# Three phases of d_ff chunks instead of two, with stores on ScalarE's queue, in a fused attention and softplus kernel

## Chip, cores, metric

One core of one Trainium2 chip. The metric is device time of one execution in microseconds, median of several runs. A single-core program gives no second core to compare with; each trace lists the granted TensorE clock.

Names: PE is TensorE, PEld its weight loads, ACT is ScalarE, DVE is VectorE, SP is SyncE (here only a queue of DMA issues). Of the tiles, `hp` takes a step's first product, `g` is its softplus, `gv` and `xv` are the three parts of g and of x, `op` takes the sums of the second product and `ot` is a copy of them; in attention `tp` is q turned (copied to `qT`), then come `kv` and `o`, and `xp` is x turned, with `xg` its scaled copy.

## The reference, cut to what matters

```python
kv  = einsum('bhsd,bhse->bhde', k, v)           # 8 batches, 8 heads, 576 rows, 64 wide
out = einsum('bhsd,bhde->bhse', q, kv)
x   = (out / rms(out) * g_norm) -> 4608 rows x 512
h   = x @ w_in                                  # 512 x 2048
g   = softplus(h)
return g @ w_out                                # 2048 x 512
```

The weights come as float64. The kernel rebuilds float32 values from their two words and carries every matmul operand as three parts, so that three matmuls stand for one in float32.

## The kernel before

36 tiles of 128 rows make 12 blocks of 384 rows. d_ff is 16 chunks of 128, in two phases of 8. One step is one chunk of one block: 12 matmuls into `hp`, softplus and split of its result on ACT and DVE, and, two steps later, 9 matmuls into three sums. All engines follow this program order.

```python
def mm1(ph, n, c):                    # 12 matmuls into hp
    ...
    nc.scalar.activation(g, hp, func=AF.Softplus, scale=1.0 + E)
    nc.scalar.activation(gv[:, 0], g, func=AF.Copy, scale=DOWN)
    nc.vector.tensor_tensor(out=gv[:, 1], in0=g, in1=f32[:, 0], op=ALU.subtract)
    nc.vector.scalar_tensor_tensor(out=gv[:, 2], ...)

def mm2(ph, n, c):                    # 9 matmuls into sums; at the last chunk of the phase:
    ...
    if ph == 0:
        ot = tmp.tile([P, d_model], F32, tag="ot", name="ot")     # 2 buffers, 3 tiles a block
        nc.scalar.activation(ot, sums[i], func=AF.Copy, scale=1.0 + E)
        nc.sync.dma_start(out=pdram[t], in_=ot)
    else: ...                         # sum + stored first sum, on DVE, to the output

def split_x(ph, t, x):                # three parts of a tile of x: ACT, DVE, DVE
    nc.scalar.activation(xv[:, 0], x, func=AF.Copy, scale=DOWN)
    nc.vector.tensor_tensor(out=xv[:, 1], in0=x, in1=f32[:, 0], op=ALU.subtract)
    nc.vector.scalar_tensor_tensor(out=xv[:, 2], ...)

def behind(step):
    mm2(*where(step - LAG))
    ...                               # i: chunk of 8; for the block that comes next
    if i in (0, 2, 4): load_x(n * TB + i // 2)
    if i in (2, 4, 6): split_x(ph, t, xts.pop(t))

def divide(j, w):                     # three parts of 128 x 512 weights
    nc.scalar.activation(dst[:, 0], w, func=AF.Copy, scale=DOWN)
    yield
    nc.vector.tensor_tensor(out=d, in0=w, in1=f32[:, 0], op=ALU.subtract)
    nc.scalar.activation(dst[:, 1], d, func=AF.Copy, scale=RADIX)
    yield
    nc.tensor.matmul(wd, lhsT=ident_r, rhs=dst[:, 0], start=True, stop=False)
    nc.tensor.matmul(wd, lhsT=minus_r, rhs=dst[:, 1], start=False, stop=True)
    nc.scalar.activation(dst[:, 2], wd, func=AF.Copy, scale=-E / (1.0 + E))

for step in range(CH, LAST):          # steps that still carry attention and conversion
    before(step)                      # mm1
    advance(heads, 1 + step % 2)      # pieces of attention: q transposed, kv, o, x transposed
    advance(weights, 1 + step % 2)    # stages of the weight conversion
    behind(step)                      # mm2, split, load
```

Attention's turned tiles of x are stored (`xg` to DRAM) and loaded again block by block (`xt`). PSUM leaves attention three places; one holds `kv`, so `xp` (x turned) and the next `tp` (q turned) want the same one.

Of the kernel before, what the change touches and what calls it, by code (L numbers as in the profile page):

```python
# [26 lines left out]
def kernel(  # L27
# [20 lines left out]

    nc = tc.nc
# [10 lines left out]
    CH = KF // 2  # L60
# [12 lines left out]
    ps_a = first_stack.enter_context(tc.tile_pool(name="ps_a", bufs=3, space=PSUM))  # L73
    att = first_stack.enter_context(tc.tile_pool(name="att", bufs=2))
    conv = first_stack.enter_context(tc.tile_pool(name="conv", bufs=1))

    ident_r = const.tile([P, P], F32R, name="ident_r")
    minus_r = const.tile([P, P], F32R, name="minus_r")
# [81 lines left out]
    def factors(j):  # L160
        c, of_out = divmod(j, 2)
        dst = wts.tile([P, 3, d_model], F32R, tag=f"w{of_out}_{c % CH}", name=f"w{of_out}_{c % CH}")
        (w_out_r if of_out else w_in_r)[c] = dst
        return dst, dst.bitcast(F32)

    def divide(j, w):
# [9 lines left out]
        wd = ps_h.tile([P, d_model], F32, tag="h", name="wd")  # L176
        nc.tensor.matmul(wd, lhsT=ident_r, rhs=dst[:, 0], start=True, stop=False)
        nc.tensor.matmul(wd, lhsT=minus_r, rhs=dst[:, 1], start=False, stop=True)  # L178
        nc.scalar.activation(dst[:, 2], wd, func=AF.Copy, scale=-E / (1.0 + E))
# [6 lines left out]
    def redivide(j):  # L186
# [4 lines left out]
        e = late.tile([P, d_model], F32, tag="e", bufs=2, name="e")  # L191
# [3 lines left out]
        yield  # L195
        nc.vector.scalar_tensor_tensor(out=e, in0=d, scalar=-RADIX, in1=f32[:, 0], op0=ALU.mult, op1=ALU.add)  # L196
        nc.scalar.activation(dst[:, 1], d, func=AF.Copy, scale=RADIX)  # L197
        yield
        nc.scalar.activation(dst[:, 2], e, func=AF.Copy, scale=-E / (1.0 + E))  # L199
# [77 lines left out]
    def turn_x(t):  # L277
# [4 lines left out]
        xg = att.tile([P, KD, P], F32, tag="xg", bufs=1, name="xg")  # L282
        nc.scalar.activation(xg, tp, func=AF.Identity, scale=g_col)  # L283
        xd[t] = dram.tile([P, KD * P], F32, name=f"x{t}")
        nc.sync.dma_start(out=xd[t], in_=xg.rearrange("p a t -> p (a t)"))
# [79 lines left out]
    def mm2(ph, n, c):  # L365
        gv, w = gvs.pop((ph, n, c)), w_out_r[c]
        first, last = c % CH == 0, c % CH == CH - 1
        for i in range(TB):
# [6 lines left out]
            if last:  # L375
                t = n * TB + i
                if ph == 0:
                    ot = tmp.tile([P, d_model], F32, tag="ot", name="ot")
                    nc.scalar.activation(ot, sums[i], func=AF.Copy, scale=1.0 + E)  # L379
                    pdram[t] = dram.tile([P, d_model], F32, name=f"part{t}")  # L380
                    nc.sync.dma_start(out=pdram[t], in_=ot)
                else:
                    ot = late.tile([P, d_model], F32, tag="ot", bufs=4, name="ot")
                    nc.vector.scalar_tensor_tensor(out=ot, in0=sums[i], scalar=scale, in1=parts_in.pop(t),  # L384
                                                   op0=ALU.mult, op1=ALU.add)
                    nc.sync.dma_start(out=out[t * P:(t + 1) * P], in_=ot)

    def load_part(t):
        parts_in[t] = late.tile([P, d_model], F32, tag="pt", bufs=3, name="pt")
        nc.sync.dma_start(out=parts_in[t], in_=pdram[t])  # L390


    HALF = n_blocks * CH
    STEPS = 2 * HALF

# [4 lines left out]
    def where(step):  # L400
        ph, r = divmod(step, HALF)
        n, c = divmod(r, CH)
        return ph, n, ph * CH + c

    def before(step):
        if step < STEPS:
            mm1(*where(step))

    def behind(step):
        if LAG <= step < STEPS + LAG:  # L410
            mm2(*where(step - LAG))

        m, i = divmod(step, CH)
        ph, n = divmod(m + 1, n_blocks)
        if ph < 2:
            if i in (0, 2, 4):
                load_x(n * TB + i // 2)
            if i in (2, 4, 6):
                t = n * TB + i // 2 - 1
                split_x(ph, t, xts.pop(t))  # L420

    for e in range(2):
        nc.sync.dma_start(out=g_col[e * D:(e + 1) * D], in_=g_norm.rearrange("(d one) -> d one", one=1))
# [5 lines left out]
    nc.vector.tensor_scalar(out=minus_r, in0=scratch, scalar1=-1.0, scalar2=None, op0=ALU.mult)  # L429
# [7 lines left out]
    weights = conversion(range(2 * CH), divide)  # L437
    advance(heads, 1)
    fetch(1)
    STARTS = {5: 0, 6: 1, 8: 2, 9: 3, 11: 4, 12: 5, 14: 6, 15: 7}  # L440
    for j in range(2 * CH):
        pieces = (3, 4, 5, 6, 6)[j] if j < 5 else 3
        for y in range(8):
            advance(weights, 1)
            if y * pieces // 8 != (y + 1) * pieces // 8:
                advance(heads, 1)
            if j in STARTS and y == 2:
                before(STARTS[j])
            if j in STARTS and y == 7:
                behind(STARTS[j])  # L450
# [3 lines left out]
    fetch(2 * CH)  # L454
    fetch(2 * CH + 1)
    weights = conversion(range(2 * CH, 4 * CH), spill)
    LAST = HALF - CH - CH
    for step in range(CH, LAST):
        before(step)
        advance(heads, 1 + step % 2)  # L460
        advance(weights, 1 + step % 2)
# [3 lines left out]


    if wide:
        ones = att.tile([P, P], F32, tag="k", bufs=3, name="ones")
        nc.vector.memset(ones, 1.0)
        nc.vector.tensor_reduce(out=scale, in_=over, axis=AX.X, op=ALU.add)  # L470
        total = ps_a.tile([P, 1], F32, tag="a", name="total")
        nc.tensor.matmul(total, lhsT=ones, rhs=scale, start=True, stop=True)
        nc.scalar.activation(scale, total, func=AF.Copy, scale=(1.0 + E) * 2.0 ** -30 / (P * 2 * KF * d_model))
    else:
# [53 lines left out]
```

## Time and profile before

| | before |
|---|---|
| runs | 1047.71 to 1053.48 us, median 1052.41 (4 runs) |
| profiled span | 1046.0 us |
| busy share PE / DVE / ACT | 92% / 50% / 41% |
| granted clock, whole span | 0.962 |

Read a busy PE with care: matmuls overlap in the trace, and at a lowered clock a busy PE does less.

### The profile page before, as it was taken

The page shows a single profiled execution, that of the slowest core. Times are in us where ns is not written, and L with a number is a line of the kernel's source. Part 1 is how long each engine was busy: PE and PEld are TensorE (multiplying, and loading weights), DVE is VectorE, ACT ScalarE, POOL GpSimd, SP SyncE. Part 2 cuts the span into 40 slices and gives each one's busy share as a digit, 9 for nine tenths or more (in the row PEclk, how much of TensorE's full clock was granted, in tenths as well). Part 3 has the DMA queues.
Part 4 walks back from the last instruction along what each step waited for, and adds up shares of the span by engine and source line. Part 5 has one row for each costly group of instructions (what it writes and reads, how often), then busy time and mean ns, then how long its engine had stood idle before and what let it go on. Part 6 is the DMA issues. An engine that isn't in the chain of part 4 may idle for free. (4 is left out here: it accounts for less than half of the span.)

```text
span 1046.0 us, 13139 instructions
## 1 busy us (share of the span) xinstructions
PE 959.1 (92%) x4994; PEld 861.4 (82%) x4994; DVE 518.5 (50%) x892; ACT 424.8 (41%) x834; POOL 88.3 (8%) x78
## 2 busy tenths in 40 slices
PE   4756768999998999989999999999999999999998
PEld 3646557898897978879898999899999999999997
DVE  3656754455464554546543457544443544444432
ACT  2546654444344443444532369333222322232221
POOL 0121112022021111113100000000000000000000
PEclk8587888999999999999999999999999999999999
DMA  9855544545555364443220333122211222022210
GB/s 220 186 151 137 139 121 121 153 121 161 143 139 143 99 161 117 126 119 104 100 65 16 101 114 108 52 90 91 81 51 51 91 91 81 25 77 91 81 61 31
DMA packets 158767, 110.18 MB, mean 105 GB/s; under 512 B 117104, under 2 KB 125296, under 8 KB 158704
## 3 DMA queue, kind: packets, MB, share of 16 engines
q1 hardware_dynamic: 158704, 109.34, 37.6%
q8 instruction: 39, 0.64, 0.3%
q14 instruction: 24, 0.20, 0.1%
HBM read 76.81 MB, written 32.51 MB: 105 GB/s over the span
## 5 line engine op out<-in xcount | busy, mean ns | idle before, releaser
L373 PE MATMUL op<-w,gv 128*128 128x512 f32 x1728 | 440.0, 398 | 11.2 <-ACT ot L379 11.2
L353 PE MATMUL hp<-xv,w 128*128 128x384 f32 x2304 | 439.5, 339 | 0.4 <-ACT g L358 0.4
L353 PEld LDWEIGHTS hp<-xv,w 128*128 128x128 f32 x2304 | 412.6, 189 | 16.6 <-ACT g L358 0.9
L373 PEld LDWEIGHTS op<-w,gv 128*128 128x128 f32 x1728 | 319.1, 189 | 73.2 <-ACT ot L379 14.2
L360 DVE TENSOR_TENSOR gv<-g,gv 128x384 fp32r<-128x384 f32 x192 | 107.1, 558 | 449.5 <-ACT gv L359 447.9
L358 ACT ACTIVATE g<-hp 128x384 f32<-128x384 f32 x192 | 94.1, 490 | 472.1 <-PE hp L353 470.6
L361 DVE SCALAR_TENSOR_TENSOR gv<-gv 128x384 fp32r<-128x384 f32 x192 | 107.2, 558 | 6.7
L359 ACT ACTIVATE gv<-g 128x384 fp32r<-128x384 f32 x192 | 100.8, 525 | 6.0
L270 POOL TENSOR_TENSOR r<-r,half 128x8 f32<-128x8 f32 x36 | 70.6, 1962 | 3.0
L240 PE MATMUL kv<-v_t,k_t 128*128 128x128 f32 (+1 forms) x320 | 55.1, 328 | 12.4 <-DMA v_t<-in_v_dram 12.4
L240 PEld LDWEIGHTS kv<-v_t,k_t 128*128 128x128 f32 (+1 forms) x320 | 51.1, 237 | 15.7 <-issue 13.8
L269 POOL TENSOR_SCALAR r<-r 128x8 f32<-128x8 f32 x36 | 17.0, 472 | 421.0 <-DVE r L268 421.0
L297 DVE SCALAR_TENSOR_TENSOR xv<-xv 128x512 fp32r<-128x512 f32 x72 | 49.8, 692 | 2.5
L262 PE MATMUL o<-kv_diag,qT 128*128 128x128 f32 (+1 forms) x320 | 46.3, 304 | 2.0 <-DVE sq L275 2.0
L296 DVE TENSOR_TENSOR xv<-xt,xv 128x512 fp32r<-128x512 f32 x69 | 47.3, 685 | 1.9 <-ACT xv L295 1.5
L262 PEld LDWEIGHTS o<-kv_diag,qT 128*128 128x128 f32 (+1 forms) x320 | 43.5, 205 | 4.1 <-DVE sq L275 2.5
L295 ACT ACTIVATE xv<-xt 128x512 fp32r<-128x512 f32 x69 | 42.8, 620 | 0.0
L178 PE MATMUL wd<-w,minus_r 128*128 128x512 f32 x16 | 10.8, 672 | 33.6 <-ACT w L174 33.6
L268 DVE TENSOR_REDUCE r<-sq 128x8 f32<-128x512 f32 x36 | 24.5, 681 | 28.8 <-ACT sq L266 28.5
L379 ACT ACTIVATE ot<-op 128x512 f32<-128x512 f32 x36 | 20.3, 593 | 43.9 <-DMA part<-ot 43.9
L251 PE MATMUL tp<-ident_r,q_t 128*128 128x128 f32 x144 | 25.5, 308 | 13.4 <-ACT xg L283 13.4
L178 PEld LDWEIGHTS wd<-w,minus_r 128*128 128x128 f32 x16 | 4.0, 250 | 38.8 <-ACT w L174 38.8
(50 smaller groups left out, 479.4 us busy)
## 6 DMA issues: line engine op xcount, KB each, us to landing
xt<-x SPq DMA_DIRECT2D x69, 256.0 KB, 2.8
x<-xg SPq DMA_DIRECT2D x36, 256.0 KB, 2.2
part<-ot SPq DMA_DIRECT2D x36, 256.0 KB, 2.2
pt<-part SPq DMA_DIRECT2D x36, 256.0 KB, 3.8
out_dram<-ot SPq DMA_DIRECT2D x36, 256.0 KB, 2.1
raw<-in_moe_w_in_dram SPq DMA_DIRECT2D x16, 512.0 KB, 4.6
k_t<-in_k_dram SPq DMA_DIRECT2D x32, 256.0 KB, 3.5
v_t<-in_v_dram SPq DMA_DIRECT2D x32, 256.0 KB, 4.2
```

Source lines behind the costliest of these rows:

```text
L240: nc.tensor.matmul(kvs[b][:, p], lhsT=kts[t][r0:r0 + n, 2 * p:2 * p + 2].rearrange("r h d -> r (h d)"), rhs=vts[t][r0:r0 + n, 2 * p:2 * p ...
L262: nc.tensor.matmul(o[r0:r0 + n, 2 * p:2 * p + 2].rearrange("r h d -> r (h d)"), lhsT=qT[:, p, r0:r0 + n], rhs=kv_diag[b % 2][:, p], start= ...
L270: nc.gpsimd.tensor_tensor(out=r, in0=r, in1=half, op=ALU.pow)
L295: nc.scalar.activation(xv[:, 0], x, func=AF.Copy, scale=DOWN)
L296: nc.vector.tensor_tensor(out=xv[:, 1], in0=x, in1=f32[:, 0], op=ALU.subtract)
L297: nc.vector.scalar_tensor_tensor(out=xv[:, 2], in0=f32[:, 1], scalar=-RADIX, in1=f32[:, 0], op0=ALU.mult, op1=ALU.add)
L353: nc.tensor.matmul(hp, lhsT=w[:, i, kd * P:(kd + 1) * P], rhs=xv[:, i, kd], start=(m == 0), stop=(m == 3 * KD - 1))
L358: nc.scalar.activation(g, hp, func=AF.Softplus, scale=1.0 + E)
L359: nc.scalar.activation(gv[:, 0], g, func=AF.Copy, scale=DOWN)
L360: nc.vector.tensor_tensor(out=gv[:, 1], in0=g, in1=f32[:, 0], op=ALU.subtract)
L361: nc.vector.scalar_tensor_tensor(out=gv[:, 2], in0=f32[:, 1], scalar=-RADIX, in1=f32[:, 0], op0=ALU.mult, op1=ALU.add)
L373: nc.tensor.matmul(sums[i], lhsT=gv[:, m, i * P:(i + 1) * P], rhs=w[:, m], start=(first and m == 0), stop=(last and m == 2))
```

## The change

The intent: PE is busy only 64% of the first 172 us, in which all eight chunks' weights of the first phase are converted. With a first phase of four chunks the steps begin earlier. Chunks 8 to 15 later take over places of the eight weight slots; 8, 9 and 12 to 15 are stored and loaded again before they do. The third phase costs another load and split of every tile of x and another store and load of sums. In passing, the third weight part moves from PE to DVE, the later division of reloaded weights works in place, and the stores of x and of the first sums are issued by ACT. The core of the diff:

```diff
-    CH = KF // 2
+    PHASES = [range(0, 4), range(4, 10), range(10, 16)]
+    PLACES = 8
@@ divide
-        wd = ps_h.tile([P, d_model], F32, tag="h", name="wd")
-        nc.tensor.matmul(wd, lhsT=ident_r, rhs=dst[:, 0], start=True, stop=False)
-        nc.tensor.matmul(wd, lhsT=minus_r, rhs=dst[:, 1], start=False, stop=True)
-        nc.scalar.activation(dst[:, 2], wd, func=AF.Copy, scale=-E / (1.0 + E))
+        nc.vector.scalar_tensor_tensor(out=w, in0=d, scalar=-RADIX, in1=f32[:, 0], op0=ALU.mult, op1=ALU.add)
+        nc.scalar.activation(dst[:, 2], w, func=AF.Copy, scale=-E / (1.0 + E))
+        yield
@@ redivide (weights stored once and loaded again)
         nc.vector.tensor_tensor(out=d, in0=w, in1=f32[:, 0], op=ALU.subtract)
-        yield
-        nc.vector.scalar_tensor_tensor(out=e, in0=d, scalar=-RADIX, in1=f32[:, 0], op0=ALU.mult, op1=ALU.add)
         nc.scalar.activation(dst[:, 1], d, func=AF.Copy, scale=RADIX)
         yield
-        nc.scalar.activation(dst[:, 2], e, func=AF.Copy, scale=-E / (1.0 + E))
+        nc.vector.scalar_tensor_tensor(out=w, in0=d, scalar=-RADIX, in1=f32[:, 0], op0=ALU.mult, op1=ALU.add)
+        nc.scalar.activation(dst[:, 2], w, func=AF.Copy, scale=-E / (1.0 + E))
@@ turn_x
-        xg = att.tile([P, KD, P], F32, tag="xg", bufs=1, name="xg")
+        xg = att.tile([P, KD, P], F32, tag="xg", name="xg")
-        nc.sync.dma_start(out=xd[t], in_=xg.rearrange("p a t -> p (a t)"))
+        nc.scalar.dma_start(out=xd[t], in_=xg.rearrange("p a t -> p (a t)"))
@@ mm2
+                if ph < len(PHASES) - 1:
+                    (nc.sync if ph else nc.scalar).dma_start(out=pdram[ph, t], in_=ot)
@@ behind (i is 0, 1, 2 at the last three chunks of a block)
-            if i in (0, 2, 4):
-                load_x(n * TB + i // 2)
-            if i in (2, 4, 6):
-                split_x(ph, t, xts.pop(t))
+            if i >= 0:
+                split_x(nph, t, xts.pop(t))
+            if -1 <= i < TB - 1:
+                load_x(nn * TB + i + 1)
@@ steps with attention
-        advance(heads, 1 + step % 2)
-        advance(weights, 1 + step % 2)
+        advance(heads, 4 if step < 14 else 3)
+        advance(weights, 2 + step % 2)
... (order of the start, places of spilled weights, scale's small matmul moved)
```

More of the change, by code (lines that the diff above doesn't have):

```diff
@@ L73 @@
     ps_a = first_stack.enter_context(tc.tile_pool(name="ps_a", bufs=3, space=PSUM))
+    conv = ctx.enter_context(tc.tile_pool(name="conv", bufs=1))
     att = first_stack.enter_context(tc.tile_pool(name="att", bufs=2))
-    conv = first_stack.enter_context(tc.tile_pool(name="conv", bufs=1))
     ident_r = const.tile([P, P], F32R, name="ident_r")
-    minus_r = const.tile([P, P], F32R, name="minus_r")
     ident = ident_r.bitcast(F32)
@@ L161, in factors @@
         c, of_out = divmod(j, 2)
-        dst = wts.tile([P, 3, d_model], F32R, tag=f"w{of_out}_{c % CH}", name=f"w{of_out}_{c % CH}")
+        dst = wts.tile([P, 3, d_model], F32R, tag=f"w{of_out}_{c % PLACES}", name=f"w{of_out}_{c % PLACES}")
         (w_out_r if of_out else w_in_r)[c] = dst
@@ L190, in redivide @@
         d = late.tile([P, d_model], F32, tag="d", bufs=2, name="d")
-        e = late.tile([P, d_model], F32, tag="e", bufs=2, name="e")
         nc.scalar.activation(dst[:, 0], w, func=AF.Copy, scale=DOWN)
@@ L366, in mm2 @@
         gv, w = gvs.pop((ph, n, c)), w_out_r[c]
-        first, last = c % CH == 0, c % CH == CH - 1
+        first, last = c == PHASES[ph][0], c == PHASES[ph][-1]
         for i in range(TB):
@@ L379, in mm2, with load_part @@
                     nc.scalar.activation(ot, sums[i], func=AF.Copy, scale=1.0 + E)
-                    pdram[t] = dram.tile([P, d_model], F32, name=f"part{t}")
-                    nc.sync.dma_start(out=pdram[t], in_=ot)
-                else:
-                    ot = late.tile([P, d_model], F32, tag="ot", bufs=4, name="ot")
-                    nc.vector.scalar_tensor_tensor(out=ot, in0=sums[i], scalar=scale, in1=parts_in.pop(t),
-                                                   op0=ALU.mult, op1=ALU.add)
-                    nc.sync.dma_start(out=out[t * P:(t + 1) * P], in_=ot)
-    def load_part(t):
-        parts_in[t] = late.tile([P, d_model], F32, tag="pt", bufs=3, name="pt")
-        nc.sync.dma_start(out=parts_in[t], in_=pdram[t])
-    HALF = n_blocks * CH
-    STEPS = 2 * HALF
+                else:
+                    ot = late.tile([P, d_model], F32, tag="ot", bufs=3, name="ot")
+                    nc.vector.scalar_tensor_tensor(
+                        out=ot, in0=sums[i], scalar=(scale if ph == len(PHASES) - 1 else 1.0 + E),
+                        in1=parts_in.pop((ph, t)), op0=ALU.mult, op1=ALU.add)
+                if ph < len(PHASES) - 1:
+                    pdram[ph, t] = dram.tile([P, d_model], F32, name=f"part{ph}_{t}")
+                    (nc.sync if ph else nc.scalar).dma_start(out=pdram[ph, t], in_=ot)
+                else:
+                    nc.sync.dma_start(out=out[t * P:(t + 1) * P], in_=ot)
+    def load_part(ph, t):
+        parts_in[ph, t] = late.tile([P, d_model], F32, tag="pt", bufs=3, name="pt")
+        nc.sync.dma_start(out=parts_in[ph, t], in_=pdram[ph - 1, t])
+    ORDER = [(ph, n, c) for ph, cs in enumerate(PHASES) for n in range(n_blocks) for c in cs]
+    BLOCKS = [(ph, n) for ph in range(len(PHASES)) for n in range(n_blocks)]
+    STEPS = len(ORDER)
+    begin = {}
+    for s, (ph, _, _) in enumerate(ORDER):
+        begin.setdefault(ph, s)
     def advance(gen, n):
@@ L398, in advance @@
             next(gen, None)
-    def where(step):
-        ph, r = divmod(step, HALF)
-        n, c = divmod(r, CH)
-        return ph, n, ph * CH + c
     def before(step):
         if step < STEPS:
-            mm1(*where(step))
+            mm1(*ORDER[step])
     def behind(step):
         if LAG <= step < STEPS + LAG:
-            mm2(*where(step - LAG))
-        m, i = divmod(step, CH)
-        ph, n = divmod(m + 1, n_blocks)
-        if ph < 2:
-            if i in (0, 2, 4):
-                load_x(n * TB + i // 2)
-            if i in (2, 4, 6):
-                t = n * TB + i // 2 - 1
-                split_x(ph, t, xts.pop(t))
+            mm2(*ORDER[step - LAG])
+        if step >= STEPS:
+            return
+        ph, n, c = ORDER[step]
+        i = c - PHASES[ph][-1] + TB - 1
+        following = BLOCKS.index((ph, n)) + 1
+        if following < len(BLOCKS):
+            nph, nn = BLOCKS[following]
+            if i >= 0:
+                t = nn * TB + i
+                split_x(nph, t, xts.pop(t))
+            if -1 <= i < TB - 1:
+                load_x(nn * TB + i + 1)
+        if ph > 0 and i >= 0:
+            load_part(ph, n * TB + i)
     for e in range(2):
-        nc.sync.dma_start(out=g_col[e * D:(e + 1) * D], in_=g_norm.rearrange("(d one) -> d one", one=1))
+        nc.scalar.dma_start(out=g_col[e * D:(e + 1) * D], in_=g_norm.rearrange("(d one) -> d one", one=1))
     fetch(0)
@@ L428 @@
     nc.vector.tensor_copy(ident_r, scratch)
-    nc.vector.tensor_scalar(out=minus_r, in0=scratch, scalar1=-1.0, scalar2=None, op0=ALU.mult)
     nc.vector.memset(half, -0.5)
@@ L436, with other @@
     heads = attention()
-    weights = conversion(range(2 * CH), divide)
+    weights = conversion(range(2 * len(PHASES[0])), divide)
     advance(heads, 1)
     fetch(1)
-    STARTS = {5: 0, 6: 1, 8: 2, 9: 3, 11: 4, 12: 5, 14: 6, 15: 7}
-    for j in range(2 * CH):
-        pieces = (3, 4, 5, 6, 6)[j] if j < 5 else 3
+    for j, (pieces, step) in enumerate(zip((2, 2, 5, 6, 6, 4, 4, 4), (None, None, None, None, None, 0, 1, 2))):
         for y in range(8):
             advance(weights, 1)
-            if y * pieces // 8 != (y + 1) * pieces // 8:
-                advance(heads, 1)
-            if j in STARTS and y == 2:
-                before(STARTS[j])
-            if j in STARTS and y == 7:
-                behind(STARTS[j])
-    advance(weights, 10 ** 6)
-    fetch(2 * CH)
-    fetch(2 * CH + 1)
-    weights = conversion(range(2 * CH, 4 * CH), spill)
-    LAST = HALF - CH - CH
-    for step in range(CH, LAST):
+            advance(heads, (y + 1) * pieces // 8 - y * pieces // 8)
+            if y == 3 and step is not None:
+                before(step)
+        if step is not None:
+            behind(step)
+    advance(weights, 10 ** 6)
+    fetch(8)
+    fetch(9)
+    def other(j, w):
+        return (divide if j // 2 < PLACES or j // 2 in (10, 11) else spill)(j, w)
+    weights = conversion(range(8, 20), other)
+    LAST = begin[1] - 5
+    for step in range(3, LAST):
         before(step)
-        advance(heads, 1 + step % 2)
-        advance(weights, 1 + step % 2)
+        advance(heads, 4 if step < 14 else 3)
+        advance(weights, 2 + step % 2)
         behind(step)
@@ L464 @@
     advance(weights, 10 ** 6)
-    if wide:
-        ones = att.tile([P, P], F32, tag="k", bufs=3, name="ones")
-        nc.vector.memset(ones, 1.0)
-        nc.vector.tensor_reduce(out=scale, in_=over, axis=AX.X, op=ALU.add)
-        total = ps_a.tile([P, 1], F32, tag="a", name="total")
-        nc.tensor.matmul(total, lhsT=ones, rhs=scale, start=True, stop=True)
-        nc.scalar.activation(scale, total, func=AF.Copy, scale=(1.0 + E) * 2.0 ** -30 / (P * 2 * KF * d_model))
-    else:
-        nc.vector.memset(scale, 1.0 + E)
     first_stack.close()
@@ L478 @@
     ps_o.append(ctx.enter_context(tc.tile_pool(name="ps_b", bufs=1, space=PSUM)))
+    weights = None
     works = []
@@ L483 @@
         before(step)
-        i = step - (HALF - CH)
-        if 0 <= i < CH:
-            reload(2 * (CH + i))
-            reload(2 * (CH + i) + 1)
+        if step == begin[1] + 8:
+            fetch(20)
+            fetch(21)
+            weights = conversion(range(20, 32), other)
+        if weights:
+            advance(weights, 1 + step % 2)
+        if step == begin[2] - 8:
+            advance(weights, 10 ** 6)
+            weights = None
+            if wide:
+                ones = late.tile([P, P], F32, tag="ot", bufs=3, name="ones")
+                nc.vector.memset(ones, 1.0)
+                nc.vector.tensor_reduce(out=scale, in_=over, axis=AX.X, op=ALU.add)
+                total = ps_h.tile([P, 1], F32, tag="h", name="total")
+                nc.tensor.matmul(total, lhsT=ones, rhs=scale, start=True, stop=True)
+                nc.scalar.activation(scale, total, func=AF.Copy, scale=(1.0 + E) * 2.0 ** -30 / (P * 2 * KF * d_model))
+            else:
+                nc.vector.memset(scale, 1.0 + E)
+        for c in (8, 9, 12, 13, 14, 15):
+            free = max(s for s, (_, _, o) in enumerate(ORDER) if o == c - PLACES)
+            if step == free + LAG - 1:
+                reload(2 * c)
+                reload(2 * c + 1)
         behind(step)
-        i -= LAG
-        if 0 <= i < CH:
-            works.append(zip(redivide(2 * (CH + i)), redivide(2 * (CH + i) + 1)))
+        for c in (8, 9, 12, 13, 14, 15):
+            free = max(s for s, (_, _, o) in enumerate(ORDER) if o == c - PLACES)
+            if step == free + LAG:
+                works.append(zip(redivide(2 * c), redivide(2 * c + 1)))
         for _ in range(2):
@@ L494 @@
                 next(gen, None)
-        n, i = divmod(step - HALF, CH)
-        if n >= 0 and i in (4, 5, 6) and n < n_blocks:
-            load_part(n * TB + i - 4)
 _INS = ['q', 'k', 'v', 'g_norm', 'moe_w_in', 'moe_w_out']
```

## The prediction

> **What bounds the kernel now.** I read four views: the busy time of each engine in stretches of the span, the waits of TensorE in two of these stretches, the timeline around one block change in the steady part, and the groups of instructions. First the stretches, cut where the program changes: the start up to the eighth converted weight piece (0 to 93.5 us), the other eight pieces (to 172.5), the steps that still carry attention work (to 517.2), and the rest. The columns are the stretch, its length, then busy us and instruction count of PE, PEld, DVE, ACT and POOL, then the granted clock, the DMA share and GB/s.
>
> ```profile
> 0.00:93.50 93.50, 54.64 (x244) 46.26 (x245) 50.65 (x91) 45.82 (x86) 14.00 (x18) 0.74 0.80 178
> 93.50:172.50 79.00, 55.80 (x273) 47.92 (x272) 46.83 (x80) 43.99 (x86) 13.16 (x11) 0.83 0.48 121
> 172.50:517.20 344.70, 324.63 (x1857) 293.53 (x1856) 179.04 (x311) 153.00 (x305) 61.12 (x49) 1.00 0.48 131
> 517.20:1046.00 528.80, 524.08 (x2625) 473.65 (x2623) 241.99 (x412) 181.96 (x357) 0.00 (x0) 1.00 0.23 73
> ```
>
> From 172.5 us on TensorE is the bound: it is busy 94% and then 99% at full clock. In the first 172.5 us nothing is full; no engine passes 71%, and the clock is at 0.74 and 0.83. Second, what TensorE waits for, before and after 172.5 us (total, times, longest):
>
> ```profile
> PE wd L178 <- ACT w L174: 33.6, 12, 5.3
> PE kv L240 <- DMA v_t<-in_v_dram: 12.4, 5, 8.5
> PE tp L251 <- ACT xg L283: 7.0, 5, 2.0
> PE wd L177 <- ACT w L169: 7.0, 4, 3.1
> ...
> PE op L373 <- ACT ot L379: 11.2, 7, 2.7
> PE tp L251 <- ACT xg L283: 6.4, 5, 1.3
> PE xp L281 <- DVE sq L275: 2.5, 1, 2.5
> ```
>
> Early, TensorE stands behind the two matmuls by which the weight conversion makes its third part (40.6 us). Later it waits 20 us in all. Third, a step of the steady part which holds a split of x (start, duration):
>
> ```profile
> 721.91 2.24 PE L373 MATMUL op<-w,gv 128*128 128x512 f32 x9
> 722.11 0.49 ACT L358 ACTIVATE g<-hp 128x384 f32<-128x384 f32 x1 [3.14 <-PE hp L353]
> 722.63 0.53 ACT L359 ACTIVATE gv<-g 128x384 fp32r<-128x384 f32 x1
> 723.07 0.62 ACT L295 ACTIVATE xv<-xt 128x512 fp32r<-128x512 f32 x1
> ...
> 724.00 2.27 PE L353 MATMUL hp<-xv,w 128*128 128x384 f32 x12
> 724.26 0.68 DVE L296 TENSOR_TENSOR xv<-xt,xv 128x512 fp32r<-128x512 f32 x1
> 724.98 0.69 DVE L297 SCALAR_TENSOR_TENSOR xv<-xv 128x512 fp32r<-128x512 f32 x1
> 725.93 1.98 PEld L373 LDWEIGHTS op<-w,gv 128*128 128x128 f32 x9
> 726.10 2.24 PE L373 MATMUL op<-w,gv 128*128 128x512 f32 x9
> ```
>
> The step repeats every 4.19 us (721.91 to 726.10): 12 matmuls into hp (2.10) and 9 into op (2.08). 192 such steps are 803.6 us that no reordering removes. Beside this stands when the split ends: 725.67, or 3.76 us after the step's hp matmuls.
>
> **What the Trainium skill says.** "TensorE: Matmul & The Clock Gate", Part 1: a TensorE left idle for a window of about 3.4 us falls to half clock. The trace agrees: in the first 172.5 us, with waits up to 8.5 us, the clock is 0.74 and 0.83, later 1.00. The same page's table gives ScalarE and VectorE strict FIFO queues; so a copy that waits holds back all behind it. The steady timeline agrees: the split on VectorE comes behind both gv operations. "DMA: Bandwidth & Descriptors", Issuing engines are not separate DMA queues: issuing from a second engine adds no bandwidth and saves issue time only. Here the gain of ScalarE's queue can therefore only be order: SyncE's queue waited 148.7 us for xg and 91.7 us for ot in the list of its own waits, and everything behind stood. No trace here issues from ScalarE yet.
>
> **The change part by part.**
>
> 1. Shorter start. Before, eight full steps' worth of chunks, sixteen pieces, are converted before step 8 begins at 172.5 us, where 7 hp groups and 5 op groups are done: 172.5 - 7*2.10 - 5*2.08 = 147.4 us that are not matrix work of the MLP. After, eight pieces and 34 pieces of attention precede step 3. By chance the old kernel has also done exactly 34 pieces of attention (1+3+4+5+6+6+3+3+3) and eight weight pieces at 93.5 us, with two hp groups. The new one has one hp and one op group more (+4.2 us), and its third weight part is made on VectorE: 8 * 0.684 = 5.5 us more there (row of L196 in the groups), while the waits for wd in this stretch, 20.5 us, go. They are in a loop DVE-ACT-PE-ACT-DVE, so I count half: 93.5 + 4.2 - 10 = 88 us. Not MLP: 88 - 3*2.10 - 2.08 = 79.6. Gain 68 us.
>
> 2. Attention moved into phase 0. After step 3 there are 148 - 34 = 114 pieces instead of 90. Before, 60 steps took 344.7 us: 344.7 - 251.2 (60 steps) - 20.1 (waits) - 2.1 (one op group of backlog) = 71.3, or 0.79 us a piece including switching. With 0.72 for the denser packing (fewer switches to and from steps; the pure spacings are 0.81, 0.81, 0.40 and 0.36 us): 114 * 0.72 = 82 us. Cost +11.
>
> 3. Waits of tp for xg. A transposition of q directly behind one of x needs its PSUM place and waited 1.3 us each time that both fell in one step. With one or two pieces a step this came 5 times after 172.5 us. With 4 or 3 pieces a step the order of pieces (x, q, kv, o, four a tile) puts the pair into one step in all 11 four-piece steps and in two of four later: about 20 times 1.3 = 26 us. Cost +20.
>
> 4. Stores from ScalarE's queue. ot no longer waits for a store stuck in SyncE's queue: the 11.2 us and the 2.5 go. Issuing took SyncE 0.32 to 0.4 us each; 72 of them add some 25 us to ScalarE over 300 us, mostly beside TensorE. I put 5 us of crowding of ScalarE and VectorE into phase 0, where pieces, conversions and splits now come together. Net -9.
>
> 5. The last split of a block. Before, splits stood at chunks 2, 4 and 6 of eight, so a whole step lay between the last and the next block. After, they stand at the last three chunks: the next block's hp matmuls follow one op group later. From the timeline: hp group over at 721.91, the next could read x at 724.00; its second four matmuls, which need L296's output, come 0.70 later (724.70), but that is ready at 724.94; [...]TensorE waits some 0.37 us. So 11 changes of phase 2 cost 4 us. In phase 1 two advances of the weight conversion stand ahead of the split in nine last steps (one or two VectorE operations of 0.42 to 0.69, ScalarE ones of 0.66 that may themselves wait for VectorE): 1.2 to 3 us each; I take 15 us. In phase 0 the same, but attention pieces give TensorE 2 to 4 us more to do: setting each split of the old kernel's first phase against the next hp group gives would-be waits of 0.06 to 2.3, mean about 1. I take 10. Cost +29.
>
> 6. The third phase itself adds 36 loads and splits of x, 36 sums stored and loaded: VectorE and ScalarE in phase 1 come to about 3 and 2 us of a 4.19 us step (1.12 gv, 0.69 split, 0.37 sums, 0.8 conversion on VectorE), DMA was at 0.23. All hidden.
>
> The sum: 88 + 189 * 4.186 (791.1) + two op groups (4.1) + 3.7 (old tail after the last op matmul) + 0.9 (the scale's small matmul) + 82 + 26 + 5 + 29 = 1030 us of span, against 1046. The runs are 2 to 7 us longer than the span (1047.91 for the profiled one, median 1053.45): I say **1034 us**, 1.8% less.
>
> **The rivals.**
>
> A: the late split is hidden or its waits overlap those of part 3, because a TensorE that waits at one place gives the others time to catch up. Then most of parts 3 and 5 goes: about 995 to 1005. For it: the designer moved these splits, and in 4-piece steps TensorE has 6 us between two hp groups. Against: the steady split ends 3.76 us after the hp group, with no load at all, and only 2.08 us are there.
>
> B: VectorE or ScalarE becomes the bound in phase 0. VectorE's work per four-piece step is 1.12 gv + 1.37 norm and sum + 1.03 split + 1.5 conversion = 5.1 of some 8.3 us, ScalarE's some 5.7 with its issues: 60 to 70%, against 52% and 44% before. With strict order and waits on each other that may cost another 20 us: 1050 to 1055, no gain. For it: at 54% and 49% in the first 93 us they already held TensorE. Against: from 172.5 us they never did for long.
>
> C: the start is bound by transfers, not by wd: the DMA share to 93.5 us is 0.80. Then step 3 begins at 98 and not at 88: 1044.
>
> **Range and chances.** The gain of part 1 (68 us) is eaten by parts 2, 3 and 5 (60 us) but for the 9 of part 4; each is known to some 10 us, the sum to some 18. Rival A is likelier than B, as such a change is rarely kept for nothing. Range 1004 to 1058. Faster by over 2% means below 1032.4, just under my figure: 0.46; within 2% 0.49; slower 0.05.
>
> **What would show it.** Right: step 3's hp group starts at 80 to 96 us; in the waits, no wd, TensorE waiting for xv of L296 and L297 (or of L295) some 30 times, 0.4 us each in the last phase; tp on xg some 20 times; op on ot nearly gone; clock 1.00 from about 100 us. Wrong: hp never waiting for xv (A), TensorE under 90% in phase 0 with VectorE or ScalarE over 75% (B), or a start that ends after 98 us with waits for loads (C).

## The result, and the profile after

| | before | after |
|---|---|---|
| median of runs | 1052.41 (4) | 1137.79 (1127.36 to 1139.79, 4) |
| ratio, 95% interval | | 1.0801, 1.0726 to 1.0875 |
| profiled span | 1046.0 | 1136.9 |
| PE busy, share of span | 959.1, 92% | 983.5, 87% |
| clock | 0.962 | 0.951 |

It is 8% slower; 1034 had been predicted. A ratio here is the mean time of one kernel's fast runs over that of the other's of the same rounds, so not quite the ratio of the medians.

First, the stretches of the kernel after, with the columns as in the prediction: the start, phase 0's steps with attention, the rest up to the last change of phase, and phase 2.

```profile
0.00:95.00 95.00, 57.32 (x281) 51.53 (x281) 57.20 (x98) 46.85 (x88) 16.14 (x20) 0.89 0.76 166
95.00:430.00 335.00, 255.39 (x1425) 225.25 (x1426) 164.83 (x276) 153.58 (x289) 69.05 (x59) 0.91 0.51 140
430.00:826.00 396.00, 365.51 (x1747) 323.01 (x1746) 227.56 (x391) 162.39 (x316) 0.00 (x0) 0.96 0.34 114
826.00:1137.00 311.00, 305.31 (x1513) 271.88 (x1511) 149.96 (x251) 92.22 (x180) 0.00 (x0) 1.00 0.27 92
```

From 95 to 430 us PE is busy 76% (255.39 of 335) at a clock of 0.91, where the kernel before had 94% at 1.00 from 172.5 us on. Yet DVE (49%) and ACT (46%) are no fuller than half. So no engine is the bound: they wait for each other. What PE waits for in 95 to 430 us:

```profile
PE tp L249 <- ACT xg L281: 42.4, 15, 8.3
PE hp L351 <- ACT xv L293: 16.8, 8, 4.2
PE o L260 <- ACT xg L281: 7.1, 4, 4.8
```

The pairs are those predicted, but a wait of tp for xg takes up to 8.3 us and not 1.3, and hp waits for the first, ACT part of the split, not just for DVE's.

To place the loss I read, in ACT's timeline, the start of the softplus of steps 3, 50, 125 and 191, and took off 4.186 us a step (the pure step of the prediction). What is left over is the excess of each stretch:

| | softplus of step 3 | excess 3 to 50 | 50 to 125 | 125 to 191 |
|---|---|---|---|---|
| before | 114.8 | 110.3 | 24.0 | 0.1 |
| after | 97.3 | 198.0 | 39.8 | 4.9 |

(In the kernel before attention lasts to step 67, so its second column is attention too.) The softplus of step 3 comes 17.5 us earlier. Its hp group comes 20.8 us earlier (91.6 for 112.4 us): in the kernel after, this softplus starts 3.45 us after the last of these matmuls, as it stands in ACT's queue. Phase 0 loses the gain four to five times over. One block change there shows how. The timeline of the kernel after, PE, ACT and DVE (start, duration, idle before):

```profile
168.79 2.27 PE L351 MATMUL hp<-xv,w 128*128 128x384 f32 x12
169.27 0.63 ACT L175 ACTIVATE w<-d 128x512 fp32r<-128x512 f32 x1 [1.95 <-DVE d L174]
170.00 0.63 ACT L178 ACTIVATE w<-w 128x512 fp32r<-128x512 f32 x1
170.54 0.58 ACT L377 ACTIVATE ot<-op 128x512 f32<-128x512 f32 x1
170.89 0.60 PE L279 MATMUL xp<-ident_r,sq 128*128 128x128 f32 x4
171.15 0.33 ACTq L385 DMA_DIRECT2D part<-ot  x1
171.52 0.60 ACT L377 ACTIVATE ot<-op 128x512 f32<-128x512 f32 x1 [0.40 <-PE xp L279]
...
175.03 0.60 ACT L377 ACTIVATE ot<-op 128x512 f32<-128x512 f32 x1 [2.91 <-DMA part<-ot]
176.03 0.63 ACT L293 ACTIVATE xv<-xt 128x512 fp32r<-128x512 f32 x1 [0.40 <-ACT ot L377]
176.57 0.47 ACT L356 ACTIVATE g<-hp 128x384 f32<-128x384 f32 x1
177.50 0.67 ACT L281 ACTIVATE xg<-xp,g_col 128x512 f32<-128x512 f32 x1
178.22 1.11 PE L249 MATMUL tp<-ident_r,q_t 128*128 128x128 f32 x4 [6.73 <-ACT xg L281]
```

hp is done at 171.06 us and xp at 171.49. Ahead of what they need, ACT has two weight copies (the first of them waits 1.95 us for DVE), then three copies of sums with a DMA issue behind each, and the third stands 2.91 us for a buffer that the first copy's store must free. Only then come the split, the softplus and xg, and PE, which needs the PSUM place that xg's copy frees, has stood 6.73 us. ACT is idle for much of that time, but its queue is strictly ordered.

### The profile page after: what moved, and what is told of

Read it like the earlier page. It is cut to its first block, busy times and chain, and to the rows that moved or that the text cites. A ratio compares the mean times of both kernels' runs of the same rounds, so it can differ in the third digit from the quotient of the medians.

```text
span 1136.9 us, 13401 instructions
## 1 busy us (share of the span) xinstructions
PE 983.5 (87%) x4962; PEld 871.7 (77%) x4962; DVE 599.6 (53%) x1015; ACT 455.0 (40%) x870; POOL 85.2 (7%) x78
## 5 line engine op out<-in xcount | busy, mean ns | idle before, releaser
L351 PE MATMUL hp<-xv,w 128*128 128x384 f32 x2304 | 461.7, 349 | 48.7 <-ACT xv L293 42.0
L351 PEld LDWEIGHTS hp<-xv,w 128*128 128x128 f32 x2304 | 420.7, 195 | 83.0 <-ACT xv L293 50.9
L371 PE MATMUL op<-w,gv 128*128 128x512 f32 x1728 | 446.3, 403 | 3.9 <-ACT ot L377 3.6
L371 PEld LDWEIGHTS op<-w,gv 128*128 128x128 f32 x1728 | 328.3, 193 | 67.1 <-ACT ot L377 5.4
L294 DVE TENSOR_TENSOR xv<-xt,xv 128x512 fp32r<-128x512 f32 x105 | 72.1, 687 | 90.0 <-ACT xv L293 89.9
L249 PE MATMUL tp<-ident_r,q_t 128*128 128x128 f32 x144 | 28.3, 331 | 61.7 <-ACT xg L281 58.8
L295 DVE SCALAR_TENSOR_TENSOR xv<-xv 128x512 fp32r<-128x512 f32 x108 | 74.7, 692 | 3.7
L293 ACT ACTIVATE xv<-xt 128x512 fp32r<-128x512 f32 x105 | 65.2, 621 | 19.8 <-DMA xt<-x 14.1
L249 PEld LDWEIGHTS tp<-ident_r,q_t 128*128 128x128 f32 x144 | 19.8, 168 | 67.6 <-ACT xg L281 63.8
L238 PE MATMUL kv<-v_t,k_t 128*128 128x128 f32 (+1 forms) x320 | 55.7, 331 | 16.4 <-DMA v_t<-in_v_dram 13.3
L377 ACT ACTIVATE ot<-op 128x512 f32<-128x512 f32 x36 | 21.3, 593 | 34.7 <-DMA part<-ot 26.4
L273 DVE TENSOR_TENSOR sq<-o,r 128x512 f32<-128x512 f32 x36 | 24.7, 686 | 14.1 <-POOL r L268 14.0
```

Of the source, the lines that this page charges most:

```text
L238: nc.tensor.matmul(kvs[b][:, p], lhsT=kts[t][r0:r0 + n, 2 * p:2 * p + 2].rearrange("r h d -> r (h d)"), rhs=vts[t][r0:r0 + n, 2 * p:2 * p ...
L295: nc.vector.scalar_tensor_tensor(out=xv[:, 2], in0=f32[:, 1], scalar=-RADIX, in1=f32[:, 0], op0=ALU.mult, op1=ALU.add)
L351: nc.tensor.matmul(hp, lhsT=w[:, i, kd * P:(kd + 1) * P], rhs=xv[:, i, kd], start=(m == 0), stop=(m == 3 * KD - 1))
L371: nc.tensor.matmul(sums[i], lhsT=gv[:, m, i * P:(i + 1) * P], rhs=w[:, m], start=(first and m == 0), stop=(last and m == 2))
```

## The experiments

All outputs are right. The ratio is to the kernel before. "Alone" edits are against the kernel after, 1.0801, whose interval is 0.0075 wide to each side (some 8 us): differences below that I read from the excess per stretch.

**Own buffer for the third copy.**

```diff
-                    ot = tmp.tile([P, d_model], F32, tag="ot", name="ot")
+                    if i < 2:
+                        ot = tmp.tile([P, d_model], F32, tag="ot", name="ot")
+                    elif n < 10:
+                        ot = att.tile([P, d_model], F32, tag="ot2", bufs=1, name="ot")
+                    else:
+                        ot = late.tile([P, d_model], F32, tag="ot", bufs=3, name="ot")
```

(and `xg` back to one buffer, for space)

> The changed kernel, but the third output copy of a block in phase 0 gets a buffer of its own (paid for by one xg buffer less). Theory 1 (FIFO): the third copy waits in ScalarE's queue for the store of the first (26.4 us in 11 waits), and the split, g and xg behind it wait too, so TensorE loses 3.5 to 8.3 us at each block change of phase 0, and then runs at half clock for a while. Expected: ot waiting for a store gone, the long waits of tp, o and op (some 37 us) down to 1.3 us each or less, phase-0 clock up, 1138 down to 1080 to 1100. Rival (density): the long waits come from the number of pieces, conversions and splits in one step, whatever the copy does; then at most 15 us.

1113.18 us, ratio 1.0574: 25 us less, fewer than expected. The waits of ot for a store are gone; the longest wait of tp for xg falls from 8.3 to 5.2 us only, and the excess of steps 3 to 50 from 198.0 to 175.8. So the wait for the store is part of the block, not all of it.

**Loads and splits of x a step earlier.**

```diff
+    for f, (nph, nn) in enumerate(BLOCKS):
+        if f > 0:
+            s0 = ORDER.index((nph, nn, PHASES[nph][0])) - TB - (f >= 3)
+            for i in range(TB):
+                split_at.setdefault(s0 + i, []).append((nph, nn * TB + i))
+                load_at.setdefault(s0 - 1 + i, []).append(nn * TB + i)
@@ behind
-            if i >= 0:
-                split_x(nph, t, xts.pop(t))
-            if -1 <= i < TB - 1:
-                load_x(nn * TB + i + 1)
+        for nph, t in split_at.get(step, ()):
+            split_x(nph, t, xts.pop(t))
+        for t in load_at.get(step, ()):
+            load_x(t)
```

> The changed kernel with loads and splits of x one step earlier, from the fourth block on, so that a whole step lies between the last split and the block that uses it. Theory 2 (late split): hp's waits for xv (47 us in 30, most of them in phases 0 and 1 where the weight conversion is ahead of the split) go, with their share of lowered clock: 1138 down to 1085 to 1105, phase 1 from 343 to about 310 us. Rival: the waits only move to another place (tp, op), less than 15 us.

1078.26 us, ratio 1.025: 60 us less, more than expected, the largest single effect. Phase 0's excess falls to 173.1, that of steps 50 to 110 from 23.8 to nothing, phase 2's from 4.9 to nothing. hp's waits for xv fall from 47.1 us to 7. The edit moves loads and splits together. In the kernel after, ACT's part of the split itself waited ten times for its load in 430 to 826 us, 12.9 us in all, so in phase 1 the share of the late split and that of the late load are not told apart.

**Other order of the pieces.**

```diff
-            while done < len(todo) and done < 5 + (t + 2) * 10 // 9:
-                next_kv()
-                yield
             if t < n_tiles:
                 rows_out(t)
                 yield
             if t > 0:
                 turn_x(t - 1)
                 yield
+            while done < len(todo) and done < 5 + (t + 2) * 10 // 9:
+                next_kv()
+                yield
```

> The changed kernel with the four pieces of attention of a tile in the order q, o, x, kv instead of q, kv, o, x, so that kv (0.89 us) stands between the transposition of x and the next one of q, which wants its PSUM place. If the short waits of tp for xg (1.3 us each) are the cost: 15 to 25 us less. If the long ones from the FIFO are: they stay and the gain is 5 to 12 us, as each is shortened by 0.9 us only.

1125.39 us, ratio 1.0693: 12 us, at the edge of noise. tp's waits fall from 58.8 to 24.9 us, but a new one, o behind the copy of q's transposition, takes 31.6. The wait moved.

**Stores back on SP's queue.**

```diff
-        nc.scalar.dma_start(out=xd[t], in_=xg.rearrange("p a t -> p (a t)"))
+        nc.sync.dma_start(out=xd[t], in_=xg.rearrange("p a t -> p (a t)"))
-                    (nc.sync if ph else nc.scalar).dma_start(out=pdram[ph, t], in_=ot)
+                    nc.sync.dma_start(out=pdram[ph, t], in_=ot)
```

> The changed kernel with the stores of x and of the first sums back on SyncE's queue. Theory 3 (issue cost): 72 issues of 0.33 us, each behind a copy, lengthen ScalarE's queue; without them 10 to 20 us faster. Theory 1 says the opposite: the store of the first copy then stands behind loads in SyncE's queue and comes later, the third copy waits longer, 20 to 60 us slower, and loads of x wait more.

1119.59 us, ratio 1.0637: 18 us less. Theory 1's fear (later stores, longer waits) did not come true: ot waits 29.9 us for stores instead of 26.4. The gain is in the range that theory 3, the cost of the issues, had given; the last section has the cost of one.

**The first three together, and slower second division.**

```diff
-        for _ in range(2):
-            for gen in works:
-                next(gen, None)
+        for gen in works:
+            next(gen, None)
```

> The three edits together (own buffer for the third copy, splits a step earlier, order q o x kv). Measured alone against the changed kernel's 1138: -25, -60, -12. If the causes are separate: their sum, 1138 - 97 = 1041, below the kernel before. If they are one and the same slack seen three times: 1065 to 1078. The wait of tp, o and op behind the third copy should be gone, the clock of phase 0 near 1.00.

> after_all3 with one round instead of two of the second division of reloaded weights in a step. In the trace of the split-early kernel steps 110 to 125 are still 13.8 us over the pure 4.19 us a step, where eight divisions fill ScalarE's queue ahead of the softplus. Expected: 8 to 13 us less than after_all3, all of it between steps 110 and 125. Rival: the excess there is the small matmul for the scale and the loads of spilled weights; then 0 to 3 us.

The three: 1060.74 us, ratio 1.0086, 77 us below the kernel after where the parts add up to 97: partly the same slack. PE's hp waits are gone, but steps 110 to 125 are still 13.8 us over. With the slower division (after_all4): 1057.78, same ratio; the 13.8 become 11.7. My reason was wrong. The timeline of this kernel (after_all4) suggests another, which the next run tests:

```profile
747.17 1.28 DVE L196 SCALAR_TENSOR_TENSOR w<-d,w 128x512 f32<-128x512 f32 x2
747.75 2.25 PE L371 MATMUL op<-w,gv 128*128 128x512 f32 x9
747.88 1.23 ACT L197 ACTIVATE w<-w 128x512 fp32r<-128x512 f32 x2 [1.82 <-DVE w L196]
748.37 1.28 DVE L193 TENSOR_TENSOR d<-w,w 128x512 f32<-128x512 f32 x2
749.09 1.23 ACT L194 ACTIVATE w<-d 128x512 fp32r<-128x512 f32 x2
750.23 1.13 ACT L191 ACTIVATE w<-w 128x512 fp32r<-128x512 f32 x2
751.26 0.47 ACT L356 ACTIVATE g<-hp 128x384 f32<-128x384 f32 x1
751.79 2.35 PE L351 MATMUL hp<-xv,w 128*128 128x384 f32 x12 [1.78 <-ACT g L356]
```

ACT's copy is placed directly behind the DVE operation that feeds it, which is itself behind gv; the softplus stands behind the copies, hp waits for its PSUM place. In the kernel before the DVE operation and its copy were a round apart.

**Both divisions decoupled,** the second, then the first:

```diff
@@ redivide
         nc.vector.tensor_tensor(out=d, in0=w, in1=f32[:, 0], op=ALU.subtract)
-        nc.scalar.activation(dst[:, 1], d, func=AF.Copy, scale=RADIX)
         yield
         nc.vector.scalar_tensor_tensor(out=w, in0=d, scalar=-RADIX, in1=f32[:, 0], op0=ALU.mult, op1=ALU.add)
+        nc.scalar.activation(dst[:, 1], d, func=AF.Copy, scale=RADIX)
+        yield
         nc.scalar.activation(dst[:, 2], w, func=AF.Copy, scale=-E / (1.0 + E))
@@ divide: the same, and the copy into dst[:, 0] one stage behind the sum that makes w;
   conversion() calls next(last, None) in its first and second stage, so that the count of stages stays
```

> The changed kernel, but the second division of reloaded weights issues ScalarE's copies one round after the VectorE operation that feeds them, as the kernel before did (still in place). Theory 4 (round trip): since the change put each copy directly behind its VectorE operation, ScalarE stands in its queue until VectorE is through, twice a step, with the softplus behind it; hp then waits for its PSUM place at steps 115 to 120. Expected: the excess of steps 110 to 125 (16.0 us in the changed kernel) down to 5 or less, 1138 down to 1124 to 1130. Rival: halving the rounds a step did not help, so it is the count of divisions and this does nothing.

> The changed kernel with the same decoupling in the first division of the weights, in the start and in phase 0 (ScalarE's three copies each come one stage after the VectorE operation that they read). ScalarE there waits 86 us for w and d of VectorE. If these waits are what delays g and xg (round trip theory): 20 to 40 us less, mostly between steps 3 and 38. If ScalarE would stand for the third copy or the late split anyway: less than 10.

after_red: 1127.78, ratio 1.0716; the excess of steps 110 to 125 falls from 16.0 to 9.2, so the round trip is about 7 us of it; not the 11 expected. What is left includes the scale's small matmul with a wait of 2.7 us and the last late split. after_div: 1120.82, ratio 1.0656, steps 3 to 50 from 198.0 to 186.6, the start 5 us shorter: 17 us, just under the range, partly in the noise.

**All five, then with stores on SP, then without the order.** (after_v5: own buffer, early split, order, both decoupled; after_v6: and stores on SP; after_v8: as v6 with the old order of pieces.)

> All five edits (own buffer for the third copy, early split, order q o x kv, both divisions decoupled), stores still from ScalarE's queue. From after_all3's 1061: 11 us at the last change of phase and 10 to 25 in the start and phase 0 less: 1025 to 1040, 1 to 2.5% under the kernel before. If the rest of phase 0 is TensorE's own work and lowered clock: 1045 to 1050.

> after_v5 with the stores of x and first sums back on SyncE's queue. On the changed kernel that gave 18 us. If the gain came from the 0.4 us that each issue with the copy before it holds ScalarE up: 8 to 15 us less than after_v5. If it came from when the stores compete with loads: no gain here, as nothing waits for the stores any more.

> after_v6 (1028) with the order of pieces put back to q, kv, o, x. The order alone gave 12 us on the changed kernel, but it moved tp's waits to o. If it still matters when ScalarE's queue is clear: 1035 to 1045. If not: within 5 us of 1028.

1043.19 (0.9906, just above the range expected), 1027.73 (0.9762), 1019.62 us (0.9714, interval 0.9697 to 0.9730). The last is 2.9% faster than the kernel before. On v5 the stores' move gave 15 us again. My expectation for v8 failed in its sign: the order that had helped costs 8 us by the medians here, 5 by the ratios, whose intervals only just part. The traces place it in the start: the softplus of step 3 comes at 100.2 us in after_v6 and at 90.5 in after_v8, while steps 3 to 50 have the same excess (123.4 and 124.6). The stretches of after_v8, cut at its own changes:

```profile
0.00:90.00 90.00, 55.75 (x299) 51.00 (x300) 58.10 (x100) 48.05 (x91) 17.42 (x20) 0.83 0.81 178
90.00:360.00 270.00, 235.94 (x1416) 211.75 (x1415) 164.62 (x275) 149.82 (x289) 67.08 (x58) 0.97 0.65 176
360.00:733.00 373.00, 369.76 (x1846) 333.88 (x1845) 236.77 (x409) 166.90 (x330) 0.00 (x0) 1.00 0.37 125
733.00:1018.00 285.00, 281.07 (x1407) 253.97 (x1406) 138.80 (x232) 83.95 (x162) 0.00 (x0) 1.00 0.27 92
```

PE is busy 87% in phase 0 and 99% behind it. The work is that of the kernel after; its order and queues differ.

**Buffer and stores alone, and copies on DVE.** (after_ot3s: the buffer edit and the stores edit; after_otdve: and `nc.vector.tensor_scalar(out=ot, in0=sums[i], scalar1=1.0 + E, scalar2=None, op0=ALU.mult)` in place of ACT's copy.)

> The changed kernel with the own buffer for the third copy and the stores back on SyncE's queue. Alone they gave 25 and 18 us. If the issues hold ScalarE's queue even when the third copy waits for nothing, they add up: 1138 down to 1092 to 1100. If both only shorten the same wait of the third copy for the first store: 1108 to 1113, as the first alone.

> after_ot3s with phase 0's copies out of the sums made by VectorE, so that nothing of a block change is left in ScalarE's queue but the split. If it is the copies and issues standing ahead of the softplus and of xg that delay the transposition of q: tp's waits longer than 2 us go and another 10 to 20 us. If what is left of those waits comes from the weight copies and the split ahead of xg: within 8 us of after_ot3s, or slower, as VectorE's gv then comes behind the copies.

1093.38 (1.0416) and 1090.96 (1.0399). Buffer and issue add up (25 and 18 give 44), so they are two causes. Waits of PE in 95 to 430 us of after_ot3s:

```profile
PE tp L249 <- ACT xg L281: 23.3, 15, 2.7
PE hp L351 <- ACT xv L293: 13.8, 7, 2.9
```

tp's waits now come to 1.6 us each, near the predicted 1.3; the longest, of 2.5 to 2.7 us, are three at block changes. Moving the copies to DVE gave 2 us, in the noise: the copies themselves are not what delays xg.

**Parts of the change on the kernel before.**

```diff
@@ before_late
-            if i in (0, 2, 4):
-                load_x(n * TB + i // 2)
-            if i in (2, 4, 6):
-                t = n * TB + i // 2 - 1
+            if i in (5, 6, 7):
+                t = n * TB + i - 5
                 split_x(ph, t, xts.pop(t))
+            if i in (4, 5, 6):
+                load_x(n * TB + i - 4)
@@ before_wd: divide as in the change;  before_q: the stores of x and first sums by nc.scalar.dma_start
```

> The kernel before with the splits of x moved to the last three chunks of a block (loads one chunk ahead), nothing else. By the would-be waits of its own trace: about 11 times 0.37 us in the second phase (4 us) and about 1 us each in the first (11 us): 1052 up to 1064 to 1072. If the late split costs what it cost the changed kernel (60 us) wherever it is put: above 1090. If conversion and attention are what make it dear: the figure above.

> The kernel before with the third weight part made on VectorE instead of by two matmuls, nothing else. Its waits for wd (40 us in the first 172) go, 11 us of VectorE's work come. I counted half of the waits as gain in the prediction: 1052 down to 1030 to 1042. If the waits were only a place where TensorE stood idle anyway: within 5 us of 1052.

> The kernel before with its stores of x and of first sums issued from ScalarE, nothing else (xg still has one buffer). The prediction gave this part 11 to 14 us of gain less 5 of crowding: op's wait for ot (11.2 us) should go, 1052 down to 1040 to 1048. If an issue costs ScalarE's queue what the changed kernel shows (0.4 us behind each copy), the gain is eaten or turned: 1052 to 1062, with op's wait smaller all the same.

before_late: 1071.03 us, ratio 1.0194 (interval 1.0175 to 1.0213, so unclear at 2%), in the range. The late split costs some 20 us in the kernel before and 60 in the kernel after. The kernel after has more block changes, so for each change it is 0.9 us (of 23) and 1.8 us (of the 33 that the early split moved). before_wd: 1042.43, ratio 0.9921, interval 0.9899 to 0.9942: 8 us, just short of the range. PE no longer waits for wd, but for xg and kv more. before_q: 1047.85, ratio 0.9984: 2 us at most. op's wait for ot falls from 11.2 to 7.5 us only, as ACT still waits 28.2 us for stores (43.9 before). So the stores' queue brings next to nothing where pieces are thin, and costs where they are dense.

## Why the prediction was wrong, by its steps

The sum had 1030 us of span; it was 1136.9. The 107 us by stretches, from the starts of the hp groups of steps 3, 50, 125 and 191 (91.6, 486.2, 843.4 and 1124.5 us): the start 4, steps 3 to 50 75, steps 50 to 125 27, the rest 1. The 75 are mostly two things. From 95 to 430 us PE stood 79.6 us (335 - 255.4), where parts 3 and 5 had put 26 + 10: 44 too few. And the sum had no term for a lowered clock, which took some 20 to 30 us there (below).

**Part 1, the start: right in kind, 4 us short.** Step 3's hp begins at 91.6 and not at 88:

```profile
91.63 2.27 PE L351 MATMUL hp<-xv,w 128*128 128x384 f32 x12
```

The waits for wd went, but in the first 95 us PE stood 16.4 us for xg before tp (3.9 in the first 93.5 of the kernel before), so that half of them counted as gain came out near by a different way than was argued. Rival C's sign, a start beyond 98 us, did not come: PE's waits for loads of q and v there are 14.4 us, 12.4 before.

**Part 2, attention's own cost: not contradicted.** (The stretch from 172.5 to 517.2 us holds 61 hp and 61 op groups, not 60 and 61; so what is left is 69 us and not 71.) In after_v8 the excess of steps 3 to 50 is 124.6, where parts 2 to 5 had put 82 + 26 + 5 + 10 = 123. That is agreement of a sum in another kernel, not of each term.

**Part 3, tp behind xg: the step that failed.** It read "waited 1.3 us each". After step 3 the pair was right and the count near (15 waits, 20 foretold), the duration was not: 42.4 us in all (the other four of the trace's 19 fell in the start, which the count left out). Nine of the 15 took 0.87 to 1.28 us, as foretold, but five, at block changes, took 3.7 to 8.3 us, 28.9 us together (one more took 2.6). I took the 1.3 from waits in which xg stood behind the softplus and gv's copy alone, as in all five of the kernel before after 172.5 us. At these block changes it stands behind copies of sums with their issues, the wait for a store and a split as well, in the timeline above behind weight copies that wait for DVE too. I had quoted that ACT's queue is strictly ordered, and had written of ACT's crowding as a share of its time. A share says nothing about a place in a queue.

**Part 4, the stores: wrong in sign.** "ot no longer waits for a store ... mostly beside TensorE, 5 us, net -9." ot did wait in ACT's queue, 26.4 us (43.9 before), since two buffers still serve three copies. PE's own wait of op for ot fell as foretold, from 11.2 to 3.6 us, but it is 1.9 us with the stores back on SP too. The own buffer gave 25 us back and the issue's removal 18, together 44. On the kernel before the move gave 2 us at most.

**Part 5, the late split: right in phase 2, too small elsewhere.** Phase 2's excess is 4.9 us against the 4 foretold (0.45 us a change; the lines of the prediction give 724.94 - 724.70 = 0.24, the rest of its 0.37 is not worked out from them). Phase 1 was given 15 us; steps 50 to 110 lost 23.8, and all of it went with the early split. In phase 0 the early split took 25 us, where I had put 10. before_late, with 20 us where the same estimate gave 15, shows that it was not far off for the kernel from which I took it: there conversion ran at 1.5 stages and attention at 1.5 pieces a step, in the new one at 2.5 and at 3 to 4.

**Part 6, "all hidden": wrong for one edit that I did not weigh.** The in-place second division put ACT's copies directly behind their DVE operations. Steps 110 to 125 lost 16.0 us, 7 of which went with the copies a round apart. The third phase's extra loads, splits and sums were hidden as predicted: in after_v8 steps 50 to 110 have an excess of 0.8 us, and steps 125 to 191 of 0.1.

**The clock.** I foretold 1.00 from 100 us. It was 0.91 from 95 to 430 us. After a long wait PE runs slowly for a while. As an estimate from that clock, (1 - 0.91) * 335 = 30 us of phase 0's time at most are lost pace, not waiting; at most, because PE also stood in part of it. PE's busy time there is 19 us above that of after_v8's phase 0 (255.39 for 235.94 us, with 1425 and 1416 instructions). I read it as a consequence of the long waits, of part 3's above all: from 95 to 430 us the clock is still 0.91 in after_split1, where hp's waits have gone and tp's reach 8.2 us, and 0.96 in after_ot3s, where no wait in that stretch passes 2.9. The trace of the kernel after shows it at the last change of phase:

```profile
820.16 4.21 PE L351 MATMUL hp<-xv,w 128*128 128x384 f32 x12 [7.14 <-ACT xv L293]
```

After a wait of 7.14 us the same 12 matmuls take 4.21 instead of 2.27 us. "TensorE: Matmul & The Clock Gate", Part 1, describes this; the trace agrees.

**The rivals.** Rival A (the waits overlap and vanish) is refuted. Rival B (ACT or DVE as the bound) named the place and the direction, but not the mechanism: neither was over half full, where it had asked for 75%. It gave 1055 at the most.

**What stays open.** The edits do not add up (97 against 77 us for three), so no cause has a price of its own. How much of phase 1's gain is the earlier load and not the earlier split is not tested, nor what the kernel before would gain from the edits of after_v8, but for before_q. With the third copy's wait and the issues gone, tp still waits for xg 1.6 us at a time; copies on DVE did not change that, and another order moved the wait to o. The first division's round trip (17 us) is measured only within the noise of the kernel after.

## What to carry to other kernels

An engine that is half idle can still be the bound: ask what stands ahead of a result in its strictly ordered queue, and which of these wait. Do not carry the duration of a wait from a kernel with thin steps to one with dense steps; rebuild the queue for the worst step, the block change. Put a copy one stage behind the operation that feeds it, keep one buffer for every copy of a burst, and finish what the next block needs a full step ahead.

## What the Trainium skill lacked or had wrong

- "DMA: Bandwidth & Descriptors", Issuing engines are not separate DMA queues: it says that issuing on several engines only saves the sequencer's issue time. No page that I read gives a figure for what an issue costs the engine that computes. Here two copies of ACT with an issue between them start 0.98 us apart (170.54 and 171.52), where the kernel before had two in 1.07 us. In the trace of the kernel after ACT stands some 0.4 us each time before a copy behind such an issue (ot nine times, 4.0 us; xv nine times, 3.6 us). Taking 72 issues off ACT gave 18 us on the kernel after and 15 on after_v5.
- "TensorE: Matmul & The Clock Gate" says in its first table that ACT and DVE are strict FIFOs. The runs agree. The page does not show how little a busy share then tells: with ACT 46% busy, PE waited 6.73 us for a 0.67 us copy.
